# Two PSUM buffers of two banks in place of one of four in the channel transforms of a two-branch FFT kernel, with a new instruction order

## The chip, the core and the metric

The program runs on one core of one Trainium2 chip. The core has five engines with a queue each: PE (TensorE, matmuls), DVE (VectorE), ACT (ScalarE), POOL (GpSimd) and SP (SyncE, which here only issues DMAs); each takes the instructions of its queue in order and stops at one whose inputs or buffers are not ready. Matmuls write to PSUM, which is declared here as one tile `banks` of 128 partitions by 8 banks of 512 fp32. The metric is the time of one execution in device microseconds; lower is better. "Within 1%" of the time before is within 2.9 us.

## The reference

Two branches over the same sequence of S = 2048 positions and D = 640 channels are mixed by a gate g that depends on the position.

```python
x = A_q
g = _sigmoid((x * gate_w).sum(-1, keepdims=True))
a = _A_ref(x, A_k, A_v, A_shift_k, A_ssm_k, A_ssm_D)
b = _B_ref(x, B_w_r, B_w_i)
return g * a + (1 - g) * b
```

Branch A: a causal convolution of `k` with 4 taps, times `v`, gives `kv`; a long causal convolution of `kv` with `ssm_k` over the sequence (by FFTs of length 2S), plus `kv * ssm_D`, times `q`. Branch B: a real 2-D FFT of `x` over sequence and channels, a product with `w_r + i w_i`, and the inverse transform.

## The kernel before

All transforms are matmuls with constant matrices in fp32. The sequence FFT has two steps (64 x 32 points), with a DVE transpose between them.

**Branch B.** The forward transform over channels is `dfwd`: for a pair of positions n, n+1 (of 16 groups) it loads `x` (one DMA of 512 KB for each), and `fold` adds and subtracts quarters of the channels: one addition of 512 elements a partition (L346), three operations of 256 (L347, L349, L350), and one of 128 (L355 with a copy by ACT, L354, or L357 alone). For positions 0 to 3 the order may put each on DVE or POOL, and so it may for the rest, except the last. Then 16 + 16 matmuls (L370, L376) write a result of four bank-sized quarters, and seven ACT operations copy it to `XX` (L386 to L393). A gate follows (`gate`), then the sequence transform (`b1` L436, `bs2` L455), the product with w (L467 to L475) and back (`i1`). The inverse over channels is `bfin`: for each n of a pair `u` (L497, L505, copied by ACT at L516), then 16 + 16 matmuls (L524, L529) with a result of four quarters again, and in `bout` for each n four ACT operations (L546, L547, L549 twice) that read the first two quarters, and two DVE operations (L552) that read the other two.

**Branch A** goes in 5 chunks of 128 channels: `kv` (the taps on ACT at L598, their sums at L604 on POOL or DVE, or the whole convolution by ACT and DVE in PSUM, L589 and L592, for chunk 0; transposes on PE at L610, the product with `v` on DVE at L618), `s1` (first step of the FFT of `kv`, "s1Y", and of the filter, "s1H": PE L635, DVE transpose L638), `amid` (second step and product: PE L671; ACT copies at L680 or L682; products at L686 on DVE or L688 on POOL), `asum` (L695, for chunks 2 to 4), `is1a` (back: PE L313, DVE transpose L318), `afin` (PE L730, times g*q at L737, and out). L646 adds `ssm_D` to one row of the filter.

**Order.** Nothing is scheduled when the program is built. Each step is recorded as an operation with its reads and writes; `TABLE` lists all 993 operations in the order in which they are issued. [...] So the table sets what stands in each engine's queue and which PSUM banks and SBUF buffers each operation gets: 11 buffers `a`, 5 buffers `s`, one `k`, 8 banks. A buffer `new("ps", n)` takes n neighbouring banks from its slot on; whoever takes a bank next waits for every operation that uses the buffer before. Slots of buffers with four banks are 0 and 4 in the table before. There are 32 such buffers: 8 of `dfwd`, 8 of `bfin`, 6 of `i1`, 10 of `is1a`. A matmul group (a `pe` operation) begins only when all its buffers are free.

Of the kernel before, what the change touches and what calls it, by code (L numbers as in the profile page):

```python
# [7 lines left out]
OP = mybir.AluOpType  # L8
# [21 lines left out]
334 139/4/2 140 143/6 144 335/4 70 339/5 340+1 341/6/0 343/4 65 67 69 68 142 141 66 71 152/0 153 158 155 154 157 156 159 36/6 37/0/1 41 38+1<37 40+1  # L30
342 39 101/7 30/8 31/4/0 32+1<31 34+1 35 94/9 323/0 344 33 79/10 42+1/4 345/0 167/2 72/1 160/3 336/5 102+1/2/3 106/0 103+1 105+1 104<105 107 328/6
324/2 95+1/4/2 99/1 96+1 43 48 46 49 44 80+1/0/1 45 47 84/0 98+1 97<98 123/8 116/7 10/9 100 325 85 326 81 83 82 73+1/4/0 77/1 327/10 78 108/4 115 109
114 113 112 111 110 346+1<73 349/2 347/0 16/0 74 76+1 75+1 86+1/4 219/1 405/0 168+1/2/3 169<168 170 171 350 413/2 348 172/2 173 161+1/4/2 162+1 164+1
165/3 87 124+1/0/1 93 92 90 88 163<124 89 91 125 127 166 225/3 427/8 329/0/0 330 337/2 338 126 128/0 129 117+1/4/0 118+1 120+1 119+1 121/1 433/10
174/4 175 180 178 181 179 176 177 17/2/3 407/6 406/4 18+1<17 19+1 245/5 409/7 122 21 351/2/1 352 20 11/4/2 12 13+1<12 14+1 353/0 354 251/0 130/4 131
133 134 135 132 136 137 408 410 15 22+1/0 23 28 26 24 29 25 434+1 357/4 358 355/6 356 27 182 183 186/4 187 188/0 189 192/2 193 194/6 195 411/9 412
428+1 4 375/4 376/4 378 377 379/0 380/6 382+1 381+1 383/2 384/0 386 385 363/6 364/7 366+1 365+1 184/4 185 190/2 416/0 418/9 422/6 191 429/0/2 430
371/4 372/7 373+1 374+1 9/0 220/6 221/1/2 246/2 222 223 224 247/3/4 248 249 250 198/0 199 200/6 201 420/1 431/4 432 414/2/0 415 226/0 417/7 419 421
232/5 400/8 227/4 228/0/1 229 230 231 359/6 360/2 361 362 435/4 436 202/2 203 395/2 252/0 367/6 253/9 368/3 387/4 284/1 388/3 254/4/2 233/2 196/0
493/0 494/4 370 369 204/6 7 389 390+1<389 499/3 437/4 495/10 255 264/0 297/9 234/3/0 423 258/6 197 235 391/0 237 497/5 504/0 438 205 393/4 496+1  # L40
424/10 236<496 498 500 303/5 257 392 265/0 394 256 285/2 286/1/0 287 289 288 401 521/3 425/4 426 396 397/6 501/7 266/1 267/3/2 268 269 270 515/10 398
399 510/0 259/2 260/4/0 261 262 263 304/4 439/0/1 440 443/6 305/1 306/1/2 307 309 308 445/2 446 298/0 299/3/0 441/4 442 402/2 502/4/0 290/6 505/2
506/1 507 444 291/6 292/5 300 301 302 463/0 403 277/4 293/4/1 294 212/9 508/1 600/0 516+1 206/5 503 464/2 466 465 455/2 456/0 458 457 459/6 460/7 296
461+1 471/4 472/3 474 473 462 475/0 476/6 478 477 295+1 467/2 468/7 470 469+1<470 404 213/4 214/6 215/2/0 451/6 452/8 454+1 207/0 208/3/1 209 522
447/4 448/4 449 450 488/7 483/5 517/2/0 518 519/0 520 601/10 453+1<522 481/4 479/0 604/8 211 216 606/6 512/9 210+1 509+1 602/1 589/0 218+1 489 511+1
704/0 482 278/4 603<511 605 607 8 480 279/1 280/4/1 281 513/6 514 271/2 590/8 525/0 526 523/2 524 527/4/1 528 533/6 529/0 530 531/2 534 591/9 592
272/4 217 273/3/0 484 485/0 593/3 594 283 282 490/6 595/6 596 532 551/2 552/2 238/1 597/4 617/9 608/3 274 239/4 276 275 486 543/0 487 491 547/6 553
554 598/2/0 240/2 241/1/4 559/4 242 544/2 546 693/6 548/8 550+1 560/0 545 539/0 540/5 611/1 599 535/2 536/3 579/4 562 492 561 609/4 549 555/6 556/2
541 542+1<541 563/0 537 610 623/4/2 243 538 629/2 558 557 625/6 624 627/4 564/8 566+1<557 630 626 565+1 318/0 628 567 319 584/10 585 244 314/4 315
312/0 313 316/4 317 310/0 311 322/0 574 569 320/4 572 321 571 573 570 580 568 575/0 576 612+1 618+1 685/0 687/5 689/3 686/2 691/7 688 690 692 675/8  # L50
696/0 700/5 698/3 697/7 699 702/3 701 703 577/4 613/0/1 621/2 578 619/4 615/6 614 581/0 622 586/2 620 616 639/4 640/2 655/6 656/0 582 647/0 648/3 587
651/2 652/9 654+1 588 642 641 643/4 583 657 658 649 650 653 694/6/0 854/0/1 852+1/2/4 644/1 645+1<653 855 705/0 695 631/6 646+1 665 666 635/4 853 706
# [168 lines left out]
def _body(ctx, tc, I, out):  # L221
# [10 lines left out]
    def new(pool, nb=1):  # L232
        return _Buf(pool, nb)
# [105 lines left out]
    def fold(n, f):  # L339
# [16 lines left out]
        else:  # L356
            op([("DVE", dvs(128), lambda: stt(fv()[:, 4], sv()[:, 3], sg, sv()[:, 2], op0=OP.mult, op1=OP.add))],  # L357
               r=[(s, 0), "two"], w=[(f, 2)], use=[s, f])
# [529 lines left out]
```

## Time and profile before

| | |
|---|---|
| time, median of 3 runs | 291.58 us (290.99 to 292.82) |
| time of the profiled execution | 290.74 us |
| its span, first to last instruction | 289.0 us |
| busy PE, DVE, POOL, ACT | 257.6, 222.4, 212.2, 150.8 us |
| mean granted TensorE clock | 0.98 |
| DMA | 53.93 MB, 187 GB/s over the span |

The profiled execution has 1.7 us outside its span, and its time lies 0.84 us below the median. PE's busy time includes 7.2 us of warming-up matmuls (L759). A busy share is a mean over stages: in the first 50 us data arrive and DVE does the folds; from 55 us on PE is nearly always busy; after 280 us only output is left. "Idle <- X" in a row means that the engine stood still before that instruction until X had ended. Line numbers are those of the kernel before; in the changed kernel lines 361 to 575 stand one higher and lines from 605 on fourteen higher.

### The profile page before, as it was taken

To read this page: it belongs to the slowest core of one execution; us is meant where nothing else is said; L and a number is where in the kernel's file an instruction comes from. 1 tells how busy PE (TensorE), PEld (TensorE's weight loads), DVE (VectorE), ACT (ScalarE), POOL (GpSimd) and SP (SyncE) were. 2 spreads that over 40 slices of the span, in tenths; PEclk is the share of its full clock that TensorE was granted. 3 is DMA by queue.
4 is the path that set the end of the run, shared out by engine and by line. 5 is a ranking of instruction groups with operands and counts; after the bars stand their busy time and mean duration, and the time that the engine had idled before them with its cause. 6 is when DMAs were issued, how large, how long until landed. Compare 5 with 4: busy or idle time off the path is not lost.

```text
span 289.0 us, 9381 instructions
## 1 busy us (share of the span) xinstructions
PE 257.6 (89%) x4024; PEld 169.9 (59%) x4024; DVE 222.4 (77%) x277; ACT 150.8 (52%) x315; POOL 212.2 (73%) x213
## 2 busy tenths in 40 slices
PE   8496899999999899789999988999998997999850
PEld 8475686555554457344575323778747674888450
DVE  1789997567999899999999999973476767365570
ACT  2237449626447435766826374355693435486420
POOL 2453646436988998686996999879892478699972
PEclk9779999999999999999999999999999999999996
DMA  6999999060368793748578943080202489306898
GB/s 237 413 344 365 346 339 362 28 248 0 103 203 315 244 300 124 221 151 296 172 232 234 424 172 100 2 270 36 85 22 73 129 173 166 41 20 77 129 123 145
DMA packets 25432, 53.93 MB, mean 187 GB/s; under 512 B 1840, under 2 KB 13360, under 8 KB 24880
## 3 DMA queue, kind: packets, MB, share of 16 engines
q1 hardware_dynamic: 22048, 48.63, 49.5%
q0 software_dynamic: 3344, 4.72, 11.9%
q8 instruction: 31, 0.51, 0.7%
q14 instruction: 9, 0.07, 0.1%
HBM read 43.38 MB, written 9.96 MB: 185 GB/s over the span
## 4 chain that ended last, share of the span: by engine, by line
PE 58%; DVE 22%; issue 4%; POOL 2%; ACT 1%; POOLq 1%; DVEq 0%; ACTq 0%
PE banks L671 9%; PE banks L635 7%; PE banks L436 7%; PE banks L529 7%; PE banks L313 6%; PE banks L497 6%; PE banks L730 5%; DVE ZZ L686 5%; DVE ZZ L638 5%; DVE ZZ L318 5%; PE banks L610 2%; PE banks L455 2%; PE banks L524 2%; DVE XX L318 2%; PE banks L370 2%
## 5 line engine op out<-in xcount | busy, mean ns | idle before, releaser
L604 POOL TENSOR_TENSOR a<-a,a 128x1024 f32<-128x1024 f32 x21 | 50.3, 2395 | 10.5 <-issue 4.1
L638 DVE STREAM_TRANSPOSE ZZ<-banks 128x1024 f32<-128x1024 f32 x40 | 47.4, 1221 | 7.7 <-PE banks L635 7.7
L598 ACT ACTIVATE a<-k,one 128x1024 f32<-128x1024 f32 x32 | 35.4, 1148 | 23.3 <-DMA k<-k 8.5
L688 POOL TENSOR_TENSOR ZZ<-a 128x512 f32<-128x512 f32 x25 | 31.7, 1286 | 18.7 <-ACT a L680 9.9
L671 PE MATMUL banks<-ZZ,s2a 64*32 64x256 f32 x1280 | 41.1, 388 | 4.1 <-DVE ZZ L686 3.2
L552 DVE SCALAR_TENSOR_TENSOR s<-banks,om,s 128x322 f32<-128x322 f32 x32 | 17.3, 551 | 22.3 <-ACT s L549 21.7
L671 PEld LDWEIGHTS banks<-ZZ,s2a 64*32 64x32 f32 x1280 | 23.2, 104 | 18.5 <-ACT s L682 4.2
L695 POOL TENSOR_TENSOR ZZ<-ZZ 128x512 f32<-128x512 f32 x23 | 28.9, 1282 | 0.4
L686 DVE TENSOR_TENSOR ZZ<-banks,s 128x512 f32<-128x512 f32 x40 | 25.3, 684 | 4.8 <-ACT s L682 3.6
L370 PE MATMUL banks<-dfc,s 128*128 128x162 f32 x128 | 21.9, 328 | 6.6 <-POOL s L349 3.8
L313 PE MATMUL banks<-ZZ,one 32*64 32x512 f32 x448 | 27.2, 606 | 0.5 <-POOL ZZ L688 0.3
L680 ACT ACTIVATE a<-banks 128x1024 f32<-128x1024 f32 x20 | 20.2, 1026 | 13.0 <-PE banks L671 10.4
L719 ACT ACTIVATE a<-a,g 128x128 f32<-128x128 f32 x80 | 24.1, 391 | 4.4 <-DMA a<-q 4.4
L318 DVE STREAM_TRANSPOSE ZZ<-banks 128x2048 f32<-128x2048 f32 x10 | 22.9, 2306 | 4.2 <-PE banks L313 4.2
L475 POOL TENSOR_TENSOR XX<-s,s 128x320 f32<-128x320 f32 (+1 forms) x29 | 24.2, 859 | 1.5 <-DVE a L604 1.2
L370 PEld LDWEIGHTS banks<-dfc,s 128*128 128x128 f32 x128 | 19.8, 207 | 9.4 <-POOL s L349 7.1
L730 PE MATMUL banks<-ZZ,is2a 128*64 128x128 f32 x320 | 19.5, 276 | 2.7 <-DVE ZZ L318 2.7
L730 PEld LDWEIGHTS banks<-ZZ,is2a 128*64 128x64 f32 x320 | 18.0, 134 | 5.9 <-DVE ZZ L318 3.6
L635 PE MATMUL banks<-a,one 64*128 64x512 f32 x80 | 19.9, 609 | 1.7 <-DVE ZZ L318 0.7
L569 POOL DMA_DIRECT2D out_dram<-a x16 | 15.6, 1393 | 7.5 <-issue 5.7
L682 ACT ACTIVATE s<-banks 128x512 f32<-128x512 f32 x20 | 12.0, 598 | 16.8 <-PE banks L671 5.8
L529 PE MATMUL banks<-dic,s 128*128 128x161 f32 x128 | 19.6, 305 | 0.8 <-DVE ZZ L318 0.8
(83 smaller groups left out, 487.1 us busy)
## 6 DMA issues: line engine op xcount, KB each, us to landing
a<-xT SPq DMA_DIRECT2D x16, 512.0 KB, 10.0
k<-k SPq DMA_DIRECT2D x10, 704.0 KB, 5.0
a<-h SPq DMA_DIRECT2D x10, 544.0 KB, 5.8
a<-w SPq DMA_DIRECT2D x16, 322.0 KB, 3.6
a<-v SPq DMA_DIRECT2D x10, 512.0 KB, 6.0
a<-q SPq DMA_DIRECT2D x10, 512.0 KB, 4.7
out_dram<-a SPq DMA_DIRECT2D x8, 512.0 KB, 4.9
out_dram<-a POOLq DMA_DIRECT2D x16, 256.0 KB, 5.7
```

The costliest lines, as they stand in the source:

```text
L313: mm(p[h * 64:h * 64 + 64, j, :nd * 8], is1[r, c, :], v[r, h * 2 + ri, :, d0:d0 + nd, :].rearrange("p m d e -> p d m e"), start=(i == 0), ...
L318: nc.vector.transpose(by_col(x, d0, nd), p[:, :, :nd * 8].rearrange("p j (d i) -> p d j i", i=8))
L370: mm(v()[:, q, i, :CB], sb(f, 5, 128)[:, x], dfc[:, x], start=first and i == 0, stop=True, skip_group_check=True)
L529: mm(v()[:, q, i, :161], sb(u, 5, 128)[:, q], dic[:, q * 161:q * 161 + 161], start=first and i == 0, stop=True, skip_group_check=True)
L598: tap = lambda t, j: op([("ACT", act_us(1024), lambda: act(sb(t, 8, 128), K(j), AF.Copy, scale=sh[:, c, j:j + 1]))], r=[k, "one"], w=[t], ...
L604: either(1024, lambda o, t=t: o(sb(acc, 1024), sb(acc, 1024), sb(t, 1024), op=OP.add), r=[t], w=[acc])
L635: mm(ps(p)[:, b], m1[r], v[r], start=True, stop=True)
L638: op([("DVE", dve(1024), lambda: nc.vector.transpose(by_col(Z(z), u * 32, 32), ps(p).rearrange("p b (d n) -> p d b n", n=16)))], r=[p], w= ...
L671: apart(c, m, "mid", mm(ps(p)[j * 32:j * 32 + 32, h].rearrange("p (y r d) -> p y r d", y=2, r=2)[:, :, ri], s2a[r, k, ri * 32:ri * 32 + 32 ...
L686: alts = [("DVE", dve(512), lambda x=x, dst=dst, hv=hv: tt(dst(), V(part(ps(p), zy)), hv(), op=OP.mult))]
L688: alts.append(("POOL", pool_us(512), lambda x=x, dst=dst, hv=hv: ptt(dst(), V(part(sb(hs, 2, 512), zy)), hv(), op=OP.mult)))
L730: mm(v[b * 64:b * 64 + 64, j, :], is2a[:, n2, :], row(Z(zh), n2), start=True, stop=True)
```

## The change

In `dfwd` and in `bfin` the result of four banks becomes two buffers of two banks, each with a slot of its own. The matmul group still takes both at its start. The operations that read the result name only the half that they read: in `dfwd` six of the seven ACT copies read the first half and one (L393) the second; in `bout` the four ACT operations of a position read the first half, and the two DVE operations (L552) the second. So each half becomes free by itself, and the two halves need not be neighbours. Sixteen buffers of four banks are left (`i1`, `is1a`); though the description lets them begin at bank 2, each has slot 0 or 4 in the new table. `kv` is written anew so that the sums of the taps could follow a plan `ADDS` (also by adding DMAs); the plan is empty, and the operations that it records are those of before, in the same order.

```diff
+ADDS = {}
 TABLE = """
-57/0 58/0/1 59 3 145/1 62/0 50/2 5 2 331/0 0 1/1 63 146+1/2/3 150/2 60+1 61+1 151 51+1/4/0 52+1 147+1 54+1 6 55/3 332/4 53<6 56 64/0 138/3 148 149 333
+57/0 0 1/0 3 5 2 50/1 145/2 331/0 138/3 339/4 36/5 94/6 58+1/0/1 30/7 101/8 59+1 62/1 61+1 79/9 63 60<61 6 51+1/2/3 55/2 52+1 53+1 56 54+1 146+1/4/0
...
     def dfwd(ns):
-        fs, p = [new("s") for _ in ns], new("ps", 4)
+        fs, p = [new("s") for _ in ns], [new("ps", 2), new("ps", 2)]
...
-        v = lambda: ps(p)[:, :, :2 * CR].rearrange("p q (i c) -> p q i c", i=2)
+        v = lambda q: ps(p[q // 2])[:, q % 2, :2 * CR].rearrange("p (i c) -> p i c", i=2)
...
-        pe(2.98, pe_, ("F", "32x128"), r=[(f, i) for f in fs for i in range(3)] + ["dfc"], w=[p], new=[p], use=fs)
+        pe(2.98, pe_, ("F", "32x128"), r=[(f, i) for f in fs for i in range(3)] + ["dfc"], w=p, new=p, use=fs)
...
-        op([("ACT", act_us(324), lambda: act(xv(0, 1), v()[:, 1, :, :CB].rearrange("p i c -> p c i"), AF.Copy))], r=[p], w=[w[4]])
+        op([("ACT", act_us(324), lambda: act(xv(0, 1), v(1)[:, :, :CB].rearrange("p i c -> p c i"), AF.Copy))], r=p[:1], w=[w[4]])
...
     def bfin(ns, is2b_buf):
-        pd = new("ps", 4)
+        pd = [new("ps", 2), new("ps", 2)]
...
-        pe(3.1, pe2, ("32x128", "F"), r=us + ["dic"], w=[pd], new=[pd])
+        pe(3.1, pe2, ("32x128", "F"), r=us + ["dic"], w=pd, new=pd)
...
-               r=[pd, "om", (ab, 0)] + ([(ab, "s"), (ab, "c", 0), (ab, "c", 1)]), w=[(ab, s)], use=[ab])
+               r=[pd[1], "om", (ab, 0)] + ([(ab, "s"), (ab, "c", 0), (ab, "c", 1)]), w=[(ab, s)], use=[ab])
```

The table is new from end to end, but PE's queue keeps its plan: the same operations, mostly swapped with neighbours. Of the operations that may run on either engine 24 go from POOL to DVE and 17 from DVE to POOL. In the stage of the folds: to DVE one addition of 512, twelve of 256 and one of a row (L646); to POOL two of 512 and six of 256. After it, up to the inverse transforms of branch B: two tap sums each way, two products of 512 each way, two sums of `bs2` (L475) each way, and one row addition (L646) to POOL. Later: two products and two sums of `asum` to DVE, one product and one subtraction of `bout` to POOL.

First place: DVE's queue at the start of the program, from the folds of position 5 (`s_75<-s_74`) on; `gs` and `dfc` are the gate's columns (L327 to L333, `gcol`), which wait for the constants `one` and `dfc`. Before:

```order
L355 TENSOR_TENSOR s_75<-s_74,banks 128x128
L346 TENSOR_TENSOR s_76<-a_64 128x512
L349 TENSOR_TENSOR s_75<-s_74 128x256
L350 TENSOR_TENSOR s_75<-s_74 128x256
L355 TENSOR_TENSOR s_77<-s_76,banks 128x128
L346 TENSOR_TENSOR s_78<-a_65 128x512
L347 TENSOR_TENSOR s_78<-a_65 128x256
L347 TENSOR_TENSOR s_76<-a_64 128x256
L350 TENSOR_TENSOR s_74<-s_78 128x256
L327 TENSOR_TENSOR gs<-one 128x4
```

The same place in the changed kernel, DVE's queue from its first fold to the last operation that the first forward transform waits for:

```order
L347 TENSOR_TENSOR s_74<-a_63 128x512
L348 TENSOR_TENSOR s_74<-a_63 128x256
L351 TENSOR_TENSOR s_75<-s_74 128x256
L356 TENSOR_TENSOR s_75<-s_74,banks 128x128
L328 TENSOR_TENSOR gs<-one 128x4
...
L347 TENSOR_TENSOR s_76<-a_64 128x512
L348 TENSOR_TENSOR s_76<-a_64 128x256
L350 TENSOR_TENSOR s_77<-s_76 128x256
L356 TENSOR_TENSOR s_77<-s_76,banks 128x128
L351 TENSOR_TENSOR s_77<-s_76 128x256
```

The first additions of position 5 come from POOL to DVE, the gate's columns go ahead of position 4 (`a_64` now, `a_65` before), and position 13 follows behind it. In SP's queue the loads of `dfc` and `one` now stand ahead of those of positions 4 and 13.

Second place: PE's queue at the end of the forward transforms over channels; the last two pairs, the transforms s1Y of chunk 0 (`kvt_62`), and the first of `b1` (`XX`). Before:

```order
L635 MATMUL banks<-kvt_62,one 128x512 x4
L370 MATMUL banks<-dfc,s_74 128x162 x4
L370 MATMUL banks<-dfc,s_75 128x162 x4
L376 MATMUL banks<-dfc,s_74 128x164 x4
L376 MATMUL banks<-dfc,s_75 128x164 x4
L376 MATMUL banks<-dfc,s_76 128x164 x4
L376 MATMUL banks<-dfc,s_77 128x164 x4
L370 MATMUL banks<-dfc,s_76 128x162 x4
L370 MATMUL banks<-dfc,s_77 128x162 x4
L635 MATMUL banks<-kvt_62,one 128x512 x4
L436 MATMUL banks<-XX,two 128x464 x12
```

PE's queue at the same place in the changed kernel:

```order
L649 MATMUL banks<-kvt_62,one 128x512 x2
L371 MATMUL banks<-dfc,s_75 128x162 x4
L371 MATMUL banks<-dfc,s_77 128x162 x4
L377 MATMUL banks<-dfc,s_75 128x164 x4
L377 MATMUL banks<-dfc,s_77 128x164 x4
L377 MATMUL banks<-dfc,s_74 128x164 x4
L377 MATMUL banks<-dfc,s_78 128x164 x4
L371 MATMUL banks<-dfc,s_74 128x162 x4
L371 MATMUL banks<-dfc,s_78 128x162 x4
L649 MATMUL banks<-kvt_62,one 128x512 x6
L437 MATMUL banks<-XX,two 128x464 x16
```

One of the four s1Y groups (two matmuls each) moves from ahead of the last two pairs to behind them, its DVE transpose with it; so three stand between the last pair and `b1` in place of two.

Third place: PE's queue in the last chunk, from the `amid` groups (`s2a`, 16 matmuls each) to the next `u` groups (`c_79`). Before:

```order
L671 MATMUL banks<-ZZ,s2a 32x2x128 x112
L497 MATMUL banks<-c_79,XX 128x2x64 x4
L505 MATMUL banks<-c_79,XX 32x64 x16
L497 MATMUL banks<-c_79,XX 128x2x64 x4
L529 MATMUL banks<-dic,s_74 128x161 x4
L529 MATMUL banks<-dic,s_76 128x161 x4
```

In the changed kernel:

```order
L685 MATMUL banks<-ZZ,s2a 32x2x128 x96
L498 MATMUL banks<-c_79,XX 128x2x64 x4
L506 MATMUL banks<-c_79,XX 32x64 x16
L498 MATMUL banks<-c_79,XX 128x2x64 x4
L530 MATMUL banks<-dic,s_77 128x161 x4
L530 MATMUL banks<-dic,s_76 128x161 x4
```

Seven `amid` groups in a row become six, in another order and with other banks: the first takes bank 6, the fifth bank 6 again, the sixth the bank of the second; before, the sixth took the bank of the third. The seventh goes behind two more inverse pairs (`dic.4` and `dic.14`) and two `u` groups, where one `amid` group stood and now two stand.

More of the change, by code (lines that the diff above doesn't have):

```diff
@@ L369, in full @@
                 for q, x in enumerate((0, 3, 2, 1)):
-                    mm(v()[:, q, i, :CB], sb(f, 5, 128)[:, x], dfc[:, x], start=first and i == 0, stop=True, skip_group_check=True)
+                    mm(v(q)[:, i, :CB], sb(f, 5, 128)[:, x], dfc[:, x], start=first and i == 0, stop=True, skip_group_check=True)
         def rest(first):
@@ L528, in full2 @@
                 for q in range(4):
[L529 removed]
+                    mm(v(q)[:, i, :161], sb(u, 5, 128)[:, q], dic[:, q * 161:q * 161 + 161], start=first and i == 0, stop=True, skip_group_check=True)
         def pe2(turn):
```

109 lines of the change are left out of this document (59 added, 50 removed).

## The prediction

> **What bounds the kernel now.** I read the page's slices first, cut the span where the limiting engine changes, and asked for each engine's busy time in those stretches. Columns: stretch in us, its length, then busy time (and instructions) of PE, its weight loads, DVE, ACT and POOL, and PE's granted clock.
>
> ```profile
> core 0: us, PE busy (x) PEld busy (x) DVE busy (x) ACT busy (x) POOL busy (x), PEclk, DMA share, GB/s
> 8.30:12.07 3.77, 0.00 (x0) 0.00 (x0) 2.86 (x13) 0.49 (x2) 0.77 (x2) 0.90 1.03 417
> 12.07:18.17 6.10, 6.10 (x34) 5.42 (x34) 4.56 (x5) 1.37 (x2) 5.22 (x8) 0.50 1.01 403
> 18.17:49.18 31.01, 26.90 (x233) 20.83 (x233) 29.70 (x49) 19.40 (x56) 15.21 (x23) 1.00 0.96 345
> 54.91:97.04 42.13, 42.12 (x664) 21.84 (x672) 35.20 (x39) 22.88 (x39) 30.21 (x24) 1.00 0.50 169
> 97.04:186.34 89.30, 81.92 (x1568) 44.96 (x1566) 87.27 (x87) 48.42 (x75) 77.09 (x59) 1.00 0.63 207
> 186.34:273.30 86.96, 84.24 (x1393) 62.70 (x1392) 52.76 (x70) 48.77 (x120) 68.78 (x84) 1.00 0.47 100
> ```
>
> Three limits follow each other. From 18 to 49 us (the folds) DVE is busy 29.70 of 31.01 us, and PE only 26.90. From 55 to 97 us PE has no hole. From 97 to 186 us DVE is busy 87.27 of 89.30 us: it leaves 2.03 us. From 186 to 273 us PE is busy 84.24 of 86.96 us: 2.72 us of holes are all that an order can win there. After 273 us the last chunk's inverse and the output follow, and the new order keeps that structure.
>
> The chain of waits says how the fold stage ends (start, duration, engine, tile, line):
>
> ```profile
> 47.34 1.24 DVE ZZ L638
> 48.57 0.56 DVE s L357
> 49.18 0.84 PE banks L376 x16
> 50.02 2.40 PE banks L370 x16
> 52.41 1.95 PE banks L635 x8
> 54.36 0.56 issue
> 54.91 1.10 PE banks L436 x4
> ```
>
> The last fold on DVE (L357) lets the last pair's transform begin at 49.18; the pair takes 3.24 us, two groups of s1Y 1.95 us, and then `b1` (L436) opens PE's long full run. Everything behind it moves by as much as `b1` moves.
>
> **The change part by part.** The sum goes against the profiled execution's 290.74 us (span 289.0 and 1.7 outside it), which lies 0.84 us below the median of the runs, 291.58; differences carry over.
>
> *The fold stage.* The prices of the moved operations, from the groups by form:
>
> ```profile
> L346 DVE TENSOR_TENSOR s<-a 128x512 f32<-128x512 f32 x14 | 10.1, 724 | 0.2 <-DMA a<-xT 0.2
> L347 DVE TENSOR_TENSOR s<-a 128x256 f32<-128x256 f32 x7 | 2.8, 411 | 0.0
> L646 DVE TENSOR_TENSOR a<-a 1x64 f32<-1x64 f32 x1 | 0.6, 604 | 0.0
> ```
>
> DVE gets one addition of 512 and gives two: -0.724. It gets twelve of 256 and gives six: 6 x 0.411 = +2.47. It gets one row addition: +0.604. Together +2.35 us on the engine that limits this stage. POOL, which loses as many, is busy 15.21 of 31.01 us there and gives nothing back by being freer. What can hide part of the 2.35 us is idle time on DVE at the start:
>
> ```profile
> 11.30 1.41 POOL L349 TENSOR_TENSOR s<-s 128x256 f32<-128x256 f32 x2 [4.80 <-DVE dfc L333]
> 11.95 1.12 ACT L589 ACTIVATE banks<-k,one 128x1024 f32<-128x1024 f32 x1 [2.31 <-DMA k<-k]
> 12.07 4.69 PE L370 MATMUL banks<-dfc,s 128*128 128x162 f32 x16 [3.78 <-POOL s L349]
> 13.10 2.61 DVE L592 SCALAR_TENSOR_TENSOR banks<-k,one,banks 128x1024 f32<-128x1024 f32 x2 [1.64 <-ACT banks L589]
> 16.69 1.48 PE L376 MATMUL banks<-dfc,s 32*128 32x164 f32 x16
> 20.02 2.47 PE L370 MATMUL banks<-dfc,s 128*128 128x162 f32 x16
> 22.41 0.84 PE L376 MATMUL banks<-dfc,s 32*128 32x164 f32 x16
> ```
>
> DVE stands still for 1.64 us until `k` has landed and ACT has read it, at 13.10. Position 5's first addition (0.72 us), now DVE's, fits in there; its followers too, but position 13's, done there before, go behind. I count 0.72 us as hidden: +1.63 us remain behind 13.10. Against this one s1Y transpose (1.24 us, the row at 47.34) leaves DVE's queue ahead of the last pair: +1.63 - 1.24 = +0.4 for that pair's start. Behind the pair PE now has three s1Y groups instead of two: 1.95 / 2 = 0.98 us more. The 0.56 us in which PE did nothing ahead of `b1` can take that much of it, as an estimate, since the last copies to `XX` run meanwhile: +0.4. So `b1` starts **0.8 us later**. Bounds: 1.6 us earlier (DVE spends its whole 1.64 us usefully and the rest goes to other gaps) and 2.35 + 0.98 = 3.3 later (nothing hidden).
>
> The first transform itself ran slow: 4.69 + 1.48 = 6.17 us at a granted clock of 0.50, against 2.47 + 0.84 = 3.31 us for the same work at 1.00. It followed 3.77 us without a matmul. Here I expect no gain, since DVE and not PE sets this stage's length.
>
> *From 55 to 97 us.* The same matmuls without a hole: nothing. DVE keeps 42.13 - 35.20 = 6.9 us of slack as cover for its reordered transposes; were it used up, each would cost at most its 1.24 us.
>
> *From 97 to 186 us.* Two tap sums, two products of 512 and two `bs2` sums go each way between DVE and POOL, equal in size, and cost nothing; POOL has 89.30 - 77.09 = 12.2 us to spare as cover. The row addition that was DVE's here is POOL's now: **-0.6 us** on the limiting engine. Bounds: 0, and -2.6 if DVE's 2.03 us of idle time went as well.
>
> *From 186 to 273 us.* PE's holes, from PE's timeline:
>
> ```profile
> 217.99 2.47 PE L529 MATMUL banks<-dic,s 128*128 128x161 f32 x16 [0.77 <-DVE ZZ L318]
> 238.40 4.78 PE L671 MATMUL banks<-ZZ,s2a 64*32 64x256 f32 x160
> 245.10 2.06 PE L671 MATMUL banks<-ZZ,s2a 64*32 64x256 f32 x64 [1.92 <-DVE ZZ L686]
> 247.09 1.22 PE L497 MATMUL banks<-c,XX 128*128 128x128 f32 x8
> 248.24 0.66 PE L505 MATMUL banks<-c,XX 128*32 128x64 f32 x32
> 248.83 1.22 PE L497 MATMUL banks<-c,XX 128*128 128x128 f32 x8
> 249.88 2.37 PE L529 MATMUL banks<-dic,s 128*128 128x161 f32 x16
> 252.18 1.39 PE L524 MATMUL banks<-dic,s 32*128 32x163 f32 x32
> ```
> ```profile
> 266.11 0.24 PEld L313 LDWEIGHTS banks<-ZZ,one 32*64 32x64 f32 x12 [0.22 <-DVE s L552]
> ```
>
> The wait at 217.99 is for the back-transpose of a four-bank buffer that stays four: it stays. At 245.10 the sixth of seven `amid` groups waits 1.92 us, as the third's bank must be read by DVE (L686) first. In the changed order six stand in a row and the sixth reuses the second's bank, which is read one group (4.78 / 5 = 0.96 us) earlier; the seventh goes away. The 0.22 us at 266.11 are a four-bank `is1a` waiting for DVE's part of `bout`; with halves it gets banks whose first half only ACT reads. Of the 1.92 + 0.22 = 2.1 us I take **-1.5**: 0.96 for sure by the earlier bank, and about half of the other 1.1. Bounds 0 and -2.1.
>
> Moving the seventh group puts its results' way behind less cover:
>
> ```profile
> L680 ACT ACTIVATE a<-banks 128x1024 f32<-128x1024 f32 x20 | 20.2, 1026 | 13.0 <-PE banks L671 10.4 <-PE banks L610 0.8 <-DMA out_dram<-a 0.7
> L682 ACT ACTIVATE s<-banks 128x512 f32<-128x512 f32 x20 | 12.0, 598 | 16.8 <-PE banks L671 5.8 <-DVE XX L439 5.0 <-POOL XX L475 4.1
> L686 DVE TENSOR_TENSOR ZZ<-banks,s 128x512 f32<-128x512 f32 x40 | 25.3, 684 | 4.8 <-ACT s L682 3.6 <-POOL XX L475 1.1
> L695 DVE TENSOR_TENSOR ZZ<-ZZ 128x512 f32<-128x512 f32 x1 | 0.7, 693 | 0.0
> ```
>
> Two ACT copies (1.03 + 0.60), four products (4 x 0.684) and two sums (2 x 0.693) make 5.75 us before `is1a` can begin. PE has beside them another `amid` group (0.96), a `bfin` pair (2.37 + half of 1.39 = 3.1) and two `u` (247.09 to 249.88: 2.8): 6.9 us. It is hidden with 1.1 us to spare; without that cover the excess is paid whole.
>
> Sum: +0.8 - 0.6 - 1.5 = -1.3 us: 290.74 - 1.3 = 289.4 for such an execution, **291.58 - 1.3 = 290.3 us** for the median.
>
> **Rivals.**
>
> *The clock stays up at the start, and it counts (faster).* PE's wait of 3.78 us is for a POOL fold (L349) which itself waited for the gate's columns (L333). Those columns stand earlier now, and their two loads too, so the first transform may begin a microsecond sooner: a gap of about 2.8 us. If the clock then stays at 1.00, the transform takes 3.31 in place of 6.17 us: -2.8. That would count if PE, not DVE, set the pace between 12 and 18 us, where DVE idles 6.10 - 4.56 = 1.54 us and PE not at all. Then 291.58 - 2.8 - 1.3 = 287.5 us. Against it: from 18 us on DVE has only 1.31 us of holes to give. [...]
>
> *DVE's queue pays for all its new folds (slower).* If the first landings move, with two loads put ahead of positions 4 and 13, DVE's early idle time comes back as waits for data; then all 2.35 us of additions stand ahead of the last pair, and the third s1Y group adds its 0.98 us: +3.3. If then the 6.9 us of cover in the last chunk or the sixth group's bank give nothing back, the -0.6 alone is left: 291.58 + 3.3 - 0.6 = 294.3; nothing of the -0.6 either, 294.9. It decides from the point where DVE has no wait left between 13 and 49 us; now it has 1.31 us after 18.17. For it: this stage is the only one where the limiting engine plainly gets more work. Against: the transpose that moves behind the pair, 1.24 us.
>
> *The halves are not felt.* Direct waits of PE for the readers of a transform's banks are few:
>
> ```profile
> PE banks L370 <- ACT XX L390: 2.7, 2, 2.3
> ```
>
> That is 2.7 us in two waits, in the stage that DVE sets. If, besides, the sixth `amid` group still waits as long, +0.8 - 0.6 = +0.2 is left: 291.8 us.
>
> **How the numbers follow.** Forecast 0.42 (290.3), the clock 0.23 (287.5), DVE pays 0.25 (294.3 to 294.9), halves not felt 0.10 (291.8). One per cent, 2.9 us, is about what a measurement can tell from no change: faster is below 288.7, slower above 294.5. Faster takes nearly all of the clock case (0.20) and the lower end of the forecast, where `b1` comes early (0.08): 0.28. Slower takes about three quarters of the DVE case, as later waits can add to its price: 0.19. Within 1%: 0.53. The range goes from 286.5 (-2.8 for the clock, -0.6, -2.1 and +0.4 for the third group) to 295.2 (the DVE case with a little behind it).
>
> **What would show it.** Right: `b1` begins at 55.7 (54.91 before), the stage 97 to 186 us is half a microsecond shorter, and the row of 1.92 us waiting for L686 is gone or below 0.9. Wrong: DVE's busy time up to the last pair's start not up by about 1 us; a first transform at a clock of 1.00 *and* an earlier `b1` (the clock rival); holes in PE between 55 and 97 us, or DVE waits there for new bank owners, which I have put at nothing; a new PE wait ahead of the last chunk's `is1a`, which would mean that the 6.9 us of cover were less.

## The result, and the profile after

The changed kernel takes **290.33 us** (median of 20 runs, 288.91 to 291.70); the kernel before, run beside it, 291.65 us (20 runs, 290.57 to 294.03). The ratio of the means is 0.9947, with a 95% interval of 0.9925 to 0.9969: 0.9 to 2.2 us faster, which is within 1%. The forecast was 290.3. Ratios here and below leave out runs that stand apart from the others of their kernel (420.56 us among the twelve of e_halves, 290.86 among the six of e_keep, one or two of the seventeen of the kernel before).

One thing has to be known before the profile is read: the profiled execution is the slowest of the twenty, 291.70 us with a span of 289.9, and so 1.0 us *longer* than the profiled execution of before (290.74). A second profile of each kernel is among the experiments.

The page's first part of the changed kernel (engine, busy us, share, instructions):

```profile
PE 258.9 (89%) x4024; PEld 169.9 (59%) x4024; DVE 225.9 (78%) x284; ACT 151.4 (52%) x315; POOL 205.8 (71%) x206
```

DVE is busy 3.5 us longer than before and POOL 6.4 us less. (A line up to 575 of the kernel before stands one higher in the changed kernel, also below 361: L346 is L347. The taps, L598, are L601, and their sums, L604, are L609.) The same kernel in the stages up to 97 us, cut where PE's work changes (columns as in the prediction: length, then busy us of PE, its loads, DVE, ACT, POOL, and the granted clock):

```profile
core 0: us, PE busy (x) PEld busy (x) DVE busy (x) ACT busy (x) POOL busy (x), PEclk, DMA share, GB/s
8.74:10.75 2.01, 0.00 (x0) 0.00 (x0) 1.67 (x6) 0.37 (x1) 0.00 (x0) 1.00 1.03 426
10.75:15.87 5.12, 5.11 (x32) 4.23 (x32) 3.76 (x6) 1.49 (x2) 3.88 (x5) 0.67 1.02 414
18.17:49.11 30.94, 26.67 (x224) 21.47 (x220) 28.20 (x54) 17.30 (x50) 13.12 (x17) 0.94 0.97 370
55.01:97.04 42.03, 40.76 (x634) 19.96 (x638) 38.15 (x41) 22.02 (x32) 33.28 (x26) 1.00 0.41 131
```

Two things differ from what the prediction said. The fold stage (the rows up to 49.11) ends at the same time although DVE was given more work. And PE, which had no hole from 55 to 97 us, now has 42.03 - 40.76 = 1.27 us of them there. The chain of waits of the changed kernel shows both (start, duration, engine, tile, line):

```profile
48.72 0.35 DVE s L358
...
49.11 0.84 PE banks L377 x16
49.95 2.40 PE banks L371 x16
52.35 2.82 PE banks L649 x12
55.17 3.34 PE banks L437 x16
...
58.61 1.15 DVE XX L440
59.76 0.53 DVE lg L405
...
60.31 2.41 DVE lg L406
...
62.92 1.07 DVE XX L440
...
64.04 3.21 PE banks L685 x87
```

The last pair starts at 49.11 (49.18 before); the third s1Y group fills the 0.56 us in which PE did nothing before, and `b1` starts at 55.01 (54.91). But then the chain leaves PE for DVE: an addition of 16 numbers a partition, L406, takes 2.4 us. It is the gate's second addition, which took 0.175 us in the kernel before, where POOL was idle from 54.1 to 58.2 us:

```profile
L405 DVE TENSOR_TENSOR lg<-lg x1: 175/175/175, 56.0 to 56.0; 128x16 f32<-128x16 f32 x1
```

The timeline of the changed kernel shows what stood beside it:

```profile
57.88 2.35 POOL L609 TENSOR_TENSOR a<-a,a 128x1024 f32<-128x1024 f32 x1
60.31 2.38 POOL L609 TENSOR_TENSOR a<-a,a 128x1024 f32<-128x1024 f32 x1
59.68 0.60 DVE L405 TENSOR_TENSOR lg<-XX 128x32 f32<-128x32 f32 x1
60.31 2.40 DVE L406 TENSOR_TENSOR lg<-lg 128x16 f32<-128x16 f32 x1
64.04 2.17 PE L685 MATMUL banks<-ZZ,s2a 64*32 64x256 f32 x64 [1.16 <-DVE XX L440]
```

POOL runs three sums of taps in a row from 55.43 on; the second ends at 60.23 and the third at 62.69. L405 ends at 60.28 and L406 at 62.71: each ends 0.02 to 0.05 us after a sum on POOL. These two additions account for 2.7 of the 3.5 us that DVE is busy longer (0.60 + 2.40 in place of 0.15 + 0.175). The two transposes behind them (L440) are late by as much, and the `amid` group that needs their banks lets PE wait 1.16 us.

### The profile page after: what moved, and what is told of

Same layout as the page of the kernel before. It is cut to its first block, busy times and chain, and to the rows that moved or that the text cites. A ratio compares the mean times of both kernels' runs of the same rounds, so it can differ in the third digit from the quotient of the medians.

```text
span 289.9 us, 9390 instructions
## 1 busy us (share of the span) xinstructions
PE 258.9 (89%) x4024; PEld 169.9 (59%) x4024; DVE 225.9 (78%) x284; ACT 151.4 (52%) x315; POOL 205.8 (71%) x206
## 4 chain that ended last, share of the span: by engine, by line
PE 64%; DVE 22%; issue 5%; ACT 3%; DMA 2%; POOL 1%; POOLq 1%; SPq 1%; ACTq 0%; DVEq 0%
PE banks L685 12%; PE banks L649 9%; PE banks L314 7%; PE banks L530 7%; PE banks L498 6%; PE banks L437 5%; PE banks L744 5%; PE banks L371 4%; DVE ZZ L652 3%; DVE XX L319 3%; DVE ZZ L319 3%; DMA a<-xT 2%; PE banks L525 2%; DVE s L468 2%; DVE ZZ L700 2%
## 5 line engine op out<-in xcount | busy, mean ns | idle before, releaser
L609 POOL TENSOR_TENSOR a<-a,a 128x1024 f32<-128x1024 f32 x21 | 50.1, 2392 | 13.7 <-ACT a L601 10.6
L601 ACT ACTIVATE a<-k,one 128x1024 f32<-128x1024 f32 x32 | 35.9, 1149 | 26.2 <-POOL a L609 9.7
L702 POOL TENSOR_TENSOR ZZ<-a 128x512 f32<-128x512 f32 x24 | 30.5, 1288 | 12.1 <-ACT a L694 10.9
L685 PEld LDWEIGHTS banks<-ZZ,s2a 64*32 64x32 f32 x1280 | 23.9, 104 | 17.5 <-issue 4.3
L700 DVE TENSOR_TENSOR ZZ<-banks,s 128x512 f32<-128x512 f32 x40 | 25.3, 682 | 6.1 <-ACT s L696 5.9
L709 POOL TENSOR_TENSOR ZZ<-ZZ 128x512 f32<-128x512 f32 x21 | 26.4, 1283 | 3.0 <-DVE ZZ L700 2.9
L371 PE MATMUL banks<-dfc,s 128*128 128x162 f32 x128 | 22.7, 335 | 4.9 <-POOL s L350 2.9
L314 PE MATMUL banks<-ZZ,one 32*64 32x512 f32 x448 | 26.6, 607 | 0.3 <-DVE XX L319 0.3
L371 PEld LDWEIGHTS banks<-dfc,s 128*128 128x128 f32 x128 | 20.4, 211 | 7.6 <-POOL s L350 3.1
L649 PE MATMUL banks<-a,one 64*128 64x512 f32 x80 | 21.1, 615 | 3.1 <-DVE ZZ L319 1.6
L649 PE MATMUL banks<-kvt,one 64*128 64x512 f32 x80 | 20.0, 616 | 0.2 <-ACT a L694 0.2
L437 PE MATMUL banks<-XX,two 64*128 64x464 f32 (+1 forms) x88 | 19.8, 582 | 0.1
```

What stands on the lines that cost most here:

```text
L314: mm(p[h * 64:h * 64 + 64, j, :nd * 8], is1[r, c, :], v[r, h * 2 + ri, :, d0:d0 + nd, :].rearrange("p m d e -> p d m e"), start=(i == 0), ...
L371: mm(v(q)[:, i, :CB], sb(f, 5, 128)[:, x], dfc[:, x], start=first and i == 0, stop=True, skip_group_check=True)
L437: mm(v()[:, b], m1b[r, ri], xv[r, ri, d0:d0 + nd], start=ri == 0, stop=ri == 1)
L601: tap = lambda t, j: op([("ACT", act_us(1024), lambda: act(sb(t, 8, 128), K(j), AF.Copy, scale=sh[:, c, j:j + 1]))], r=[k, "one"], w=[t], ...
L609: either(1024, lambda o: o(sb(ts[x], 1024), sb(ts[x], 1024), sb(ts[y], 1024), op=OP.add), r=[ts[y]], w=[ts[x]])
L649: mm(ps(p)[:, b], m1[r], v[r], start=True, stop=True)
```

## The experiments

All runs are compared by where four groups stand in PE's timeline: `b1`, the first inverse of chunk 0 (`is1a`), the row of `amid` groups of chunk 3 at about 186 us, and the last `afin`. The table gives the start of `b1` and the lengths to each next one; it shows where a kernel gains or loses within one execution, to a few tenths of a microsecond.

| kernel | b1 starts | to first is1a | to amid, chunk 3 | to last afin | span | median of runs |
|---|---|---|---|---|---|---|
| before | 54.91 | 34.68 | 96.68 | 89.69 | 289.0 | 291.65 |
| before_again | 54.97 | 34.62 | 96.51 | 89.69 | 289.6 | 291.38 (one) |
| after | 55.01 | 36.37 | 96.53 | 88.73 | 289.9 | 290.33 |
| after_again | 54.62 | 36.47 | 96.25 | 87.28 | 288.6 | 290.38 (one) |
| e_halves | 55.29 | 34.68 | 96.37 | 91.85 | 291.0 | 291.96 |
| e_gate | 54.56 | 34.61 | 96.13 | 87.36 | 285.5 | 287.64 |
| e_pool | 54.47 | 36.23 | 96.22 | 88.14 | 289.0 | 290.13 |
| e_oldhead | 54.48 | 34.58 | 95.91 | 88.32 | 287.3 | 288.06 |
| e_late | 54.32 | 34.60 | 96.09 | 87.61 | 285.5 | 286.92 |
| e_late_again | 53.23 | 34.57 | 96.34 | 87.48 | 285.1 | 287.76 |
| e_keep | 54.98 | 34.57 | 95.81 | 87.57 | 286.0 | 287.59 |
| e_tail | 54.13 | 34.69 | 96.49 | 93.93 | 293.4 | 295.31 |
| e_tail2 | 54.28 | 34.70 | 96.01 | 89.05 | 286.9 | 289.38 |

Beside the runs of the experiments the kernel before had medians of 291.2 to 291.3 us.

### A second profile of both kernels

> The changed kernel once more, unchanged, for a second profile. The profile on hand is of a run of 291.70 us, 1.37 above the kernel's median; in it PE stands still for 1.31 us at 246.08 in the last chunk with no releaser, one matmul short of the end of the fifth amid group. Theory 1 (that hole belongs to that one run): here it is absent and the span is about 288.6. Theory 2 (it is a wait of the new order): it is there again, 1.0 to 1.5 us. Both expect the gate's second addition (L406) on DVE at about 2.4 us again, since three tap sums run on POOL beside it.

> The kernel before once more, for a second profile. The 1.92 us wait of the sixth amid group for DVE (L686) is there again (a rule of the order), and the first transform is slow again (6.1 us, granted clock about 0.5); if either is an accident of one run, it is below half of that here.

PE's timeline of the changed kernel, first profile:

```profile
239.97 4.80 PE L685 MATMUL banks<-ZZ,s2a 64*32 64x256 f32 x159
246.08 1.29 PE L685 MATMUL banks<-ZZ,s2a 64*32 64x256 f32 x33 [1.31 <-issue]
```

and second profile:

```profile
239.48 5.87 PE L685 MATMUL banks<-ZZ,s2a 64*32 64x256 f32 x192
```

The six groups run through without a hole the second time, and the span is the 288.6 us expected by theory 1: 1.31 us of the first profile's span were that execution's. Most other runs with the new last chunk have a hole of 0.2 to 0.9 us there; in one of them (e_oldhead, 0.88 us) the profile names DVE's products (L700) as the releaser. So the hole varies from execution to execution, and what causes it is not shown. L406 took 2.40 us in both profiles, and the stage from `b1` to `is1a` was 36.4 and 36.5 us: that loss belongs to the order. In the kernel before, the wait of 1.92 us came again (1.87), and the first transform was again slow (4.69 us for its first part).

### The gate moved

```diff
-... 184/2 358 406/8 356 411/9 408<14 354 192/4 193 416/0 413/2 410 188/6 182 186/0
+... 184/2 182 358 406/8 356 411/9 408<14 354 192/4 193 416/0 413/2 410 188/6 186/0
```

In an entry `+1` takes the second of two engines, the numbers behind the slashes are the slots of new buffers, and `<j` adds a wait for operation j. Operation 182 is the gate's three additions, 358, 356 and 354 are the s1Y transposes, 193 the first transpose of `b1`, and 408, 410 and a later 412 the three sums on POOL.

> The changed kernel with one operation moved: the gate's three additions on DVE go ahead of the three s1Y transposes in place of behind them and the first b1 transpose, so that they run before POOL's three tap sums begin. Theory 1 (DVE's L406 was held for 2.4 us by POOL's tap sum, and the 1.16 us that PE then waited at 64.04 in its full stretch is lost for good): L406 takes under 0.3 us, the wait at 64 us is gone, and the time is 1.0 to 1.5 us below the changed kernel's 290.3, so 288.8 to 289.3. Theory 2 (the DVE-bound stage behind absorbs it): the wait is gone, but the time is within 0.4 us of 290.3.

The timeline of this kernel:

```profile
53.47 0.19 DVE L405 TENSOR_TENSOR lg<-XX 128x32 f32<-128x32 f32 x1 [4.19 <-ACT XX L393]
53.70 0.18 DVE L406 TENSOR_TENSOR lg<-lg 128x16 f32<-128x16 f32 x1
54.99 7.28 POOL L609 TENSOR_TENSOR a<-a,a 128x1024 f32<-128x1024 f32 x3 [8.11 <-ACT a L601]
61.29 3.89 PE L685 MATMUL banks<-ZZ,s2a 64*32 64x256 f32 x128
```

The additions have ended 0.9 us before POOL begins, PE's `amid` row has no wait, and the stage takes 34.61 us in place of 36.4: 1.8 us, which is the wait of 1.16 and what the late transposes cost the groups behind it. Nothing behind gives it back. The median is 287.64 us (ratio to the kernel before 0.9893, 0.9846 to 0.9941). Against the changed kernel's 290.33 that is 2.7 us, but the kernel before took 291.17 us beside this run and 291.65 beside that one; by the ratios (0.9893 against 0.9947) the two lie 1.6 us apart, about the 1.8 of the stage. The mechanism of theory 1 holds. The time lies below the 288.8 to 289.3 that it expected, since it counted the wait of 1.16 us alone.

### The same collision taken away from the other side

```diff
-... 411/9 408<14 354 192/4 193 416/0 413/2 410 188/6 182 186/0
+... 411/9 354 192/4 193 416/0 188/6 182 408<182 410 413/2 186/0
```

> The changed kernel with the gate left where it is in DVE's queue, and the first two of POOL's three tap sums made to wait for the gate in its stead (so the load of v that reuses their buffer comes later too). Theory 1 (POOL's tap sums held DVE's two-input additions): L405 and L406 take about 0.2 us each, PE's wait of 1.16 us at 64 us is gone, b1 to the first is1a takes about 34.7 us as in the kernel before and not 36.4, and the time is 287.5 to 289.3. Theory 2 (it was the gate's place behind the first b1 transpose that delayed the next ones): the additions are short, but b1 to is1a stays above 35.5 us and the time near 290.3.

The timeline of this kernel:

```profile
59.32 0.18 DVE L406 TENSOR_TENSOR lg<-lg 128x16 f32<-128x16 f32 x1
59.84 7.36 POOL L609 TENSOR_TENSOR a<-a,a 128x1024 f32<-128x1024 f32 x3 [13.06 <-issue]
64.78 1.02 ACT L694 ACTIVATE a<-banks 128x1024 f32<-128x1024 f32 x1 [1.68 <-POOL a L609]
67.22 1.02 ACT L694 ACTIVATE a<-banks 128x1024 f32<-128x1024 f32 x1 [0.93 <-POOL a L609]
67.76 1.99 PE L437 MATMUL banks<-XX,two 64*128 64x480 f32 x8 [0.82 <-DVE ZZ L700]
```

The additions came out as theory 1 said, the stage and the time as theory 2 said: L406 takes 0.18 us again beside an idle POOL, so it was POOL that held it; and yet the stage takes 36.23 us, and the median is 290.13 us (ratio 0.9967, 0.9935 to 1.0000). But not for the reason of theory 2: the next transposes of `b1` begin at 59.65, as early as in e_gate (59.75). The sums now begin 4.4 us later, ACT's copies of the first `amid` groups wait for the buffers that the sums still use (1.68 + 0.93 us), DVE's products wait for ACT, and PE for DVE. POOL must begin early, so the gate has to go ahead of it.

### The halves alone

```diff
-22+1/0 ... 130/4
+22+1/0/2 ... 130/4/6
```

(so for all sixteen results, on the kernel before with the changed kernel's two buffers).

> The kernel before with the two buffers of two banks in place of one of four and nothing else: every pair of halves gets the neighbouring banks that the one buffer had, the order and the engines are those of before. The forecast's rival 'the halves are not felt': 291.4 to 291.8, PE's wait for the ACT copies ahead of the forward transforms (2.7 us in two waits) stays near 2.7. If freeing a half early is what the change lives on: 290.3 to 290.8 and that wait is halved.

291.96 us, ratio 1.0029 (0.9993 to 1.0065): no gain that can be measured. PE's wait for the ACT copies fell from 2.7 to 2.2 us, far from halved. By itself, freeing a half early shows no gain here. Its long last stage, 91.85 us, is known from one profile only: the wait of the sixth group was 2.50 us in place of 1.92, and the 64 `amid` matmuls behind it took 3.62 us at a granted clock of 0.53, in place of 2.06. The run has one more use. Its first transform ran at full speed, and its third did not:

```profile
12.15 2.47 PE L371 MATMUL banks<-dfc,s 128*128 128x162 f32 x16 [2.64 <-POOL s L350]
23.96 4.14 PE L371 MATMUL banks<-dfc,s 128*128 128x162 f32 x16
```

The first took 2.47 us in place of 4.69, in the same order, and `b1` came no earlier (55.29 against 54.91). But the third took 4.14 us (granted clock 0.59) in place of 2.47, so the run does not show that the clock is without effect in this stage.

### The old fold stage

This is the kernel before up to the gate (with halves in neighbouring banks), then the order of e_gate, with buffers renamed from the seam on.

> The kernel before up to the gate (with halves in neighbouring banks), and from there the changed kernel's order: everything new but the fold stage, and no tap sum of POOL beside the gate. Theory 1 (the new fold stage is worth a few tenths, in spite of 2.35 us more work on DVE): 0.2 to 0.6 us above the run with the gate moved (287.6), so 287.8 to 288.3, b1 at 54.9. Theory 2 (the additions cost the 0.8 us forecast, and that run lies low by luck): b1 no later than in that run, and the time equal to it or below.

Measured 288.06 us (ratio 0.9884, 0.9837 to 0.9930), `b1` at 54.48. That run and e_gate (287.64, `b1` at 54.56) can't be told apart, neither in the time nor in the stage. The time lies in the range of theory 1, `b1` where theory 2 had it. The times alone, with intervals of almost 3 us each, don't exclude the 0.8 us that I forecast; the start of `b1` speaks against it: 54.1 to 55.3 us in the six profiles with the old fold stage, 54.5 to 55.0 in the four with the new one (mean 54.7 in both).

### The early constants put back

```diff
-57/0 0 1/0 3 5 2 50/1 145/2 331/0 ... 60<61 6 51+1/2/3 55/2 52+1 53+1 56 54+1 146+1/4/0
+57/0 0 1/0 3 50/1 145/2 5 2 331/0 ... 60<61 51+1/2/3 55/2 52+1 53+1 56 54+1 6 146+1/4/0
```

> The run with the gate moved, and in it the loads of the constants one and dfc put back behind those of positions 4 and 13, and the gate's columns back behind position 4's folds on DVE, as in the kernel before. Theory 1 (the early columns pay for DVE's additions: the first transform begins 1.5 us sooner, which lets DVE's later folds start sooner): the first transform at about 12, b1 at 55.3 or later, the time 0.7 to 1.5 us above 287.6. Theory 2 (from 18 us on DVE alone sets the stage and the start is hidden): first transform at about 12 but b1 at 54.4 to 54.8 and the time within 0.4 of 287.6.

Both theories expected the first transform at about 12, and both were wrong in that. The two profiles of this kernel, the second from a later run of it (e_late_again); of each the first transform and the one near 29 us:

```profile
10.32 3.67 PE L371 MATMUL banks<-dfc,s 128*128 128x162 f32 x16 [1.97 <-DVE dfc L330]
28.30 4.14 PE L371 MATMUL banks<-dfc,s 128*128 128x162 f32 x16 [2.89 <-POOL s L350]
```
```profile
10.38 2.47 PE L371 MATMUL banks<-dfc,s 128*128 128x162 f32 x16 [1.07 <-DVE dfc L330]
28.89 2.47 PE L371 MATMUL banks<-dfc,s 128*128 128x162 f32 x16 [2.96 <-POOL s L350]
```

The first transform begins at 10.3 without the early constants. What had kept it until 12.07 in the kernel before was that POOL had the pair's last folds and stood behind the gate's columns; now DVE does those folds while the constants are still on their way, and only the columns are waited for. The time is 286.92 us (ratio 0.9841, 0.9787 to 0.9896) in the first run and 287.76 (0.9893, 0.9834 to 0.9951) in the second: no worse than e_gate, so no gain from putting the constants ahead can be seen. The same kernel's `b1` stands at 54.32 and 53.23: the transform near 29 us took 4.14 us in the first profile (granted clock 0.65 up to the end of the pair) and 2.47 in the second (1.00).

### The last chunk alone

> The kernel before up to the pair of positions 8 and 9 of the inverse over channels (with halves in neighbouring banks), and from there the changed kernel's order and banks: the new last chunk alone. Forecast of the prediction: 1.5 us less than before, bounds 0 and 2.1. Theory 1 (the last chunk's holes are worth all that they measure, 1.9 + 0.2 us or a little more): 2.0 to 2.5 us below the kernel before, from the five-group amid row to the last afin 87.4 us in place of 89.7. Theory 2 (the gain needs the earlier stages of the new order): under 1 us.

295.31 us, 4 us *slower* than before, which neither theory expected. The timeline of this kernel:

```profile
242.89 0.41 POOL L556 TENSOR_TENSOR a<-s 128x128 f32<-128x128 f32 x1 [5.36 <-DMA out_dram<-a]
244.52 0.60 ACT L696 ACTIVATE s<-banks 128x512 f32<-128x512 f32 x1 [5.17 <-POOL a L556]
246.59 1.96 PE L685 MATMUL banks<-ZZ,s2a 64*32 64x256 f32 x32 [4.35 <-DVE ZZ L700]
```

At the seam POOL's subtraction for the output of position 8 or 9 got a buffer that an output DMA was still reading; ACT waited for POOL, DVE for ACT, and the sixth `amid` group for DVE: 4.35 us. The splice made its own wait, and the run says nothing on the question. The second try cuts earlier, at about 205 us, where the buffers that meet have long been free:

> The last chunk alone once more, now spliced earlier: the kernel before up to the inverse pair of positions 6 and 7 (about 205 us; with halves in neighbouring banks), and from there the changed kernel's order, banks and buffers; the first splice, at 232 us, let POOL wait 5.4 us for an output DMA that was still reading a buffer. Theory 1 (the new last chunk is worth what its holes measured): no long wait of the amid groups, from the five-group row of chunk 3 (186 us) to the last afin 87.4 us in place of 89.7, time 2.0 to 2.6 us below the kernel before. Theory 2 (the gain needs the earlier stages): under 1 us.

```profile
203.05 1.14 PE L649 MATMUL banks<-kvt,one 64*128 64x512 f32 x4 [0.79 <-ACT s L517]
243.49 1.29 PE L685 MATMUL banks<-ZZ,s2a 64*32 64x256 f32 x33 [0.82 <-issue]
```

The stage takes 89.05 us, and 87.4 without the 0.79 us at the seam and the varying hole of 0.82. The median is 289.38 us, ratio 0.9946 (0.9912 to 0.9980), 0.6 to 2.6 us below before; the two theories' bounds, 1 and 2 us, both lie inside. The fair partner is e_halves, whose table is the same up to the seam: its ratio is 1.0029 (0.9993 to 1.0065), and the two intervals don't meet. So the last chunk gains by itself; how much, these runs don't tell closely.

### Matmuls that keep PE busy ahead of the last afin

```diff
+    unit("keep")
+    pk = new("ps", 2)
+
+    def hold():
+        for _ in range(6):
+            mm(ps(pk)[:, 0, :128], wrm, wrm, start=True, stop=True)
+
+    pe(1.8, hold, "F", r=["wrm"], w=[pk], new=[pk])
```

> The run with gate moved and loads put back, and six more matmuls on zeros (1.8 us, into a bank that is free by then) in the 2.8 us in which PE waits ahead of the last afin. In five of the ten profiles so far these last 64 matmuls took 5.3 to 5.5 us in place of 3.85. Theory 1 (the wait lets the clock fall in some runs): 3.85 us always, and the median 0.3 to 1.0 us below that run's 286.9. Theory 2 (nothing behind PE is late by it, or the added matmuls delay it): the same median or above.

> The run with the gate moved and the two loads and the gate's columns put back, unchanged, as what e_keep is compared with on the same chip: 286.6 to 288.2, the last afin either 3.85 or about 5.4 us.

The kernel with the added matmuls (six calls, which the profile records as twelve) and the one without, last `afin` of each:

```profile
270.67 1.60 PE L838 MATMUL banks<-wrm 128*128 128x128 f32 x12 [0.45 <-ACT s L550]
272.93 3.85 PE L744 MATMUL banks<-ZZ,is2a 128*64 128x128 f32 x64 [0.66 <-DVE ZZ L319]
```
```profile
271.62 5.45 PE L744 MATMUL banks<-ZZ,is2a 128*64 128x128 f32 x64 [2.81 <-ACT a L733]
```

3.85 us against 5.45 in these two profiles (granted clock 1.00 and 0.69), but the medians are 287.59 and 287.76 us, with ratios of 0.9875 and 0.9893 that overlap widely. One profile with 3.85 us is no proof, since seven profiles have it without the added matmuls. (The expectation's five of ten profiles was a miscount: at that time it was four.) From the start of these matmuls to the end of the span it is 12.8 to 13.8 us in the seven quick profiles without the added matmuls and 13.5 to 14.2 in the five slow ones, so up to a microsecond may hang on it. Whether the added matmuls bring it stays open.

**The best of these versions** are the changed kernel with the gate moved (e_gate) and the same with the constants put back (e_late): 286.9 to 287.8 us, 1.1 to 1.6% below the kernel before. The versions with the new last chunk and without the collision (e_gate, e_oldhead, e_late twice, e_keep) have ratios of 0.984 to 0.989, the changed kernel 0.9947 and e_pool 0.9967.

## Why the prediction was right

The number was right to a few hundredths, 290.3 against 290.33, and that closeness is luck: by the second profile of each kernel the four terms were missed by -1.2, +1.9, +0.3 and -0.9 us, and these cancel. Two of the signs that the prediction had named for being wrong came true: DVE's busy time up to the last pair's start did not rise, and PE has a hole between 55 and 97 us. The part on the last chunk was right in its mechanism.

**The fold stage (+0.8 forecast).** Over the profiles the start of `b1` has moved by nothing that can be told from the spread (54.9 and 55.0 before, 55.0 and 54.6 after), and e_oldhead says the same. The step that failed is "together +2.35 us on the engine that limits this stage". Up to the last pair's start DVE's busy time went *down*, from 1.88 + 2.86 + 4.56 + 29.70 = 39.00 us to 2.65 + 1.67 + 3.76 + 1.41 + 28.20 = 37.69 (the stretches from 0 to 49.11, the first and the fourth not shown above). I had counted +2.35 - 1.24 = +1.1, so 2.4 us are missing. The groups up to 49.2 us say about where; the kernel before, with one of its four operations and what POOL did beside it, then the changed one:

```profile
L357 DVE SCALAR_TENSOR_TENSOR s<-s,two 128x128 f32<-128x128 f32 x4 | 2.8, 699 | 0.7 <-PE banks L376 0.6
44.12 0.89 DVE L357 SCALAR_TENSOR_TENSOR s<-s,two 128x128 f32<-128x128 f32 x1
44.14 0.73 POOL L347 TENSOR_TENSOR s<-a 128x256 f32<-128x256 f32 x1 [2.42 <-PE banks L376]
```
```profile
L358 DVE SCALAR_TENSOR_TENSOR s<-s,two 128x128 f32<-128x128 f32 x4 | 1.9, 467 | 0.0
L660 DVE TENSOR_TENSOR a<-a 1x64 f32<-1x64 f32 x1 | 0.3, 252 | 0.0
L347 DVE TENSOR_TENSOR s<-a 128x512 f32<-128x512 f32 x13 | 9.1, 697 | 3.9 <-DMA a<-xT 3.9
```

Four folds of one kind take 0.9 us less together: beside a fold on POOL one takes 0.44 to 0.89 us (all four before, one after), beside an idle POOL 0.34 (three after). The row addition that I priced at 0.604 takes 0.252, beside an idle POOL too, and the additions of 512 take 0.3 us less than counted. And two of the new folds of 256, 0.41 us each, stand *behind* the operation that lets the last pair start; PE's second part of it (L371, at 49.95) begins after both have ended:

```profile
48.98 0.41 DVE L350 TENSOR_TENSOR s<-s 128x256 f32<-128x256 f32 x1
49.32 0.41 DVE L351 TENSOR_TENSOR s<-s 128x256 f32<-128x256 f32 x1
```

0.9 + 0.35 + 0.3 + 0.8 makes about the 2.4 (an estimate, since the records of neighbours overlap by some hundredths). I had read the count of the moved operations from the table, but neither their place relative to the launch nor how long they take once POOL does less beside them. That the third s1Y group fills the 0.56 us of nothing was right.

But DVE's sum is not the whole of it. In all seven profiles with the new fold stage `b1` begins 21.2 us (21.16 to 21.27) after the start of the matmuls that follow the transform near 29 us (L649, at 33.84 in the changed kernel); with the old stage and the old order behind it this takes 22.1 us in five profiles. So behind that point the new order is 0.9 us shorter, while ahead of it the transform ran slow in six of the seven (3.3 to 4.1 us at a granted clock of 0.64 to 0.69, in place of 2.47), and PE's next matmuls and `b1` came later by as much. That `b1` did not move is itself a balance. The prediction's premise that DVE and not PE sets this stage's length does not hold for the new fold stage from 29 us on.

**From 55 to 97 us (nothing forecast).** Wrong by +1.8 us: 34.7 us became 36.4. The prediction named holes here as what would make it wrong, but its cover, DVE's 6.9 us of slack, was the wrong one to count. The slack is a sum over the stage; the wait came from one addition held at one place, and PE has none to give back. The step that failed is that I checked how much work moved in this stage and not what now runs *beside* what: the gate went behind the first `b1` transpose, into POOL's three sums. e_gate shows the size and e_pool the holder.

**From 97 to 186 us (-0.6 forecast).** Too large, and the sign is barely told from the spread: 96.0 to 96.7 us in the five profiles with the old order here (mean 96.4), 95.8 to 96.5 in the eight with the new one (96.2), so -0.2.

**The last chunk (-1.5 forecast, bounds 0 and -2.1).** The mechanism was right: the wait of 1.92 us for the third group's bank is gone in the second profile and replaced by 0.2 to 1.3 us in most others, and the 0.22 us at `is1a` is gone. The stage went from 89.69 to 88.73 and 87.28 us, -1.0 and -2.4, the second a little beyond the bound, and the moved group's results stayed hidden. That the new chunk gains by itself is shown by e_tail2 beside e_halves.

**The rivals.** The clock rival failed on its own condition: PE's gap became 2.01 us, shorter than the 2.8 I gave it, and the clock was still down (0.67 from 10.75 to 15.87). The first transform of the changed kernel:

```profile
10.75 3.81 PE L371 MATMUL banks<-dfc,s 128*128 128x162 f32 x16 [2.01 <-DVE s L350]
14.49 1.38 PE L377 MATMUL banks<-dfc,s 32*128 32x164 f32 x16
```

5.19 us in place of 3.31. No run shows that a gap of 2.8 us keeps the clock at 1.00 there, the condition of the rival's -2.8 us: gaps of 2.64 and 2.72 us were followed by 2.47 us for the transform's first part, gaps of 2.89 and 2.97 by 3.56 and 3.89. Yet the rival's second half, that the clock counts in this stage, has something in it, at another place than it named: the transform near 29 us, whose clock the prediction did not consider, ended 1.1 us earlier in the second profile of e_late, and `b1` came 1.1 us earlier. The rival that the halves are not felt is half right: alone they are not (e_halves). The new order of the last chunk uses halves that are no neighbours; whether an equally good order with whole fours exists was not tried. The slower rival named the wrong place but about the right kind of loss: a DVE operation at a spot where nothing behind is slack.

The stage lengths of the profiles need not add up to the medians' difference of 1.3 us: with the second profile of each kernel they give -0.35 + 1.85 - 0.26 - 2.41 = -1.2 to the last `afin`, with the first pair only +0.1 + 1.7 - 0.15 - 0.96 = +0.7. Which of the two is typical is told by the twenty runs, not by the profiles.

## What to carry to other kernels

Before costing what an edit adds to an engine, ask what will run beside it: the gate's second addition, 0.18 us beside an idle POOL (e_gate, e_pool), took 2.40 us beside a sum of 2.38 us on POOL, and did so at a place where the next buffers are freed. Read a moved operation's place relative to the instruction that is waited for, not just its stage: two of the new folds, 0.41 us each, stood behind it. Look at each transform's own duration in the timeline, not only at the busy sums: one that runs slow can set a stage that another engine seems to limit, as the one near 29 us did in the first profile of e_late, with 4.14 us in place of 2.47 and `b1` 1.1 us later than in the second. And take two profiles before explaining a difference of a microsecond: of the two of the changed kernel only the first has the hole of 1.31 us.

## What the runs showed of the hardware

**The held addition shows as busy, not as waiting.** L406 of the changed kernel has no idle time before it and 2.40 us of busy time for 16 numbers a partition, against 0.18 us in e_gate and e_pool; both L405 and L406 end within 0.05 us of the end of a sum on POOL. In the profile nothing names POOL; the only signs are the odd duration and the common end. The price in these runs: beside one whole tap sum, 2.38 us, an addition of 0.18 us took 2.40.

**Gaps of 1.8 to 3.0 us did not always leave the clock up.** Ahead of the first transform, gaps of 3.78 and 4.07 us (the two profiles of the kernel before) were followed by 4.69 us for its first 16 matmuls; 2.97 us by 3.89 (e_tail); 2.89 by 3.56 (e_tail2); 2.30 by 4.40 (e_gate); 2.01 by 3.81 and 1.77 by 3.62 (the two of the changed kernel); 1.97 by 3.67 (e_late); but 2.72 (e_oldhead) and 2.64 (e_halves) by 2.47, full speed. The shorter gaps of 1.07 (e_late_again) and 1.22 (e_keep) were followed by 2.47, and 1.17 (e_pool) by 2.73. (Granted clocks: 0.50 behind the gap of 3.78 and 0.67 behind that of 2.01.) Ahead of the transform near 29 us of the new fold stage, gaps of 2.88 to 2.96 us were followed by 2.47 us in one profile and by 3.3 to 4.1 in six. Ahead of the last `afin`, the same gap of 2.8 us was followed by 3.85 to 3.88 us in seven profiles (three of them with the old last chunk, where it was 2.7) and by 5.3 to 5.5 us in five. So the length of the gap alone does not decide; what does is not shown.
